# A Fourier layer and a maxout feed-forward on one core: when the last batch's z is split and inverted, and how its sums are spread over the steps

## The chip, the core and the metric

The kernel runs on one core of a Trainium2 chip. The metric is the device time of one execution in microseconds (us): median 1740.72 of three runs, lowest 1739.53, highest 1741.87.

## What is computed

x has shape (8, 3072, 256). Each batch goes through a real Fourier transform along its 3072 positions, a complex 256 x 256 product with bias, a soft threshold of 0.01 and the inverse transform. The 24576 rows that result go through a maxout feed-forward of width 768.

```python
X = np.fft.rfft(x, axis=1)
Yr, Yi = Xr @ w_r - Xi @ w_i + b_r, Xr @ w_i + Xi @ w_r + b_i
Y = soft(Yr, 0.01) + 1j * soft(Yi, 0.01)
y = np.fft.irfft(Y, n=3072, axis=1).reshape(24576, 256)
h = np.maximum(np.maximum(y @ w1, y @ w2), y @ w3)
out = h @ w_out
```

## The kernel before, in words

**Numbers in two halves.** [...] A float32 operand is split into a high half (ScalarE, `activation` with Copy) and a low half (VectorE, operand minus high half), and a product is made of three matmuls: high x high, high x low, low x high.

**Loops.** The main loop (L1427 to L1489) runs over 8 batches b, 8 units c in each, and 6 steps f in each unit. A unit is a tile of y: 384 positions (4 columns n2 times 96) of 256 features, held as `yh` and `yl`. A step makes 128 of the 768 hidden features of one unit. Beside the steps of batch b, the Fourier stages of later batches run out of a list of `events` with due times; by the last batch (b = 7, the only one in `SEVEN`) there is none of that left.

**From z to y.** The spectrum of a batch lies in DRAM as `z_d`. `load_z` (L1013) brings a unit's part to the tile `zq` (one buffer). `split_z` (L1052) makes the halves `zh` (L177, ScalarE) and `zl` (L178, VectorE) and then has SP copy them between partitions to the two tiles `ze` (L1068): four copies of 48 KB for each piece, and two pieces for a unit of the last batch. `inverse` (L1078) multiplies `ze` with tables: 16 short matmuls to `pi` (L1092) for each of the two halves of the features (h = 0, 1). ScalarE copies the even half to `ye` (L1100), VectorE makes `y32` with two instructions (`halves`, L1106), ScalarE its high half `yh` (L1111) and VectorE the low one `yl` (L1113).

**Seven products in the last batch.** There the two products with w1 and w2 of a step are made of seven quarter-size products (`seven_a`, L1179, and its `part_b`, `part_c`, `part_d`). Four of them take sums of quarters of y: `sums` (L1122) makes t1 to t4 with four subtractions (L1127) in the tile `ty`, converts them in one instruction of 768 elements (L1128, ScalarE) and takes their low halves in one (L1129, VectorE).

**One step of the last batch on TensorE**, in the order in which it is written; "last" is the step before:

- `seven_a`: three matmuls `pf<-y`, three `pf<-ty`; ScalarE copies them out of PSUM (L1190, L1192)
- three matmuls of `down` (`pd<-hh`) for an older step
- `part_c` of the last step: six `pu<-ty`; then VectorE adds (L1203) and ScalarE applies Relu (L1208)
- three matmuls of `down`
- `part_b`: three `pu<-ty`, three `pf<-y`; ScalarE copies (L1197)
- three matmuls of `down`
- `part_d` of the last step: three `pu<-yh` that add to what L1203 has read; then VectorE (L1214, twice), ScalarE (L1220) and VectorE (L1221) make the halves `hh` of the hidden features

In three steps of a unit, `down` also takes six matmuls of y itself (`pd<-gh,yh`).

**What is asked for when.** A step has four points at which `flush` (L154) lets the functions run that were put off with `later`; a function put off at one point runs at the next. In the last batch, the split of the next unit's z is asked for in step 0 after `seven_a`, both pieces at once (L1436); the first half of the inverse at the end of step 3 (L1466), the second in step 4 after `part_b` (L1458). `halves`, `parts` and `sums` follow at the next points, one after the other; t1 to t4 and their conversion stand at the first point of step 5, all together. At the start of a batch (c = 0 of the next batch, `late`) the split is asked for in step 2 and the first inverse in step 4. `in_turn` (L163) keeps an instruction behind the last L1208 (ScalarE) and the last L1214 (VectorE) asked for so far.

The framework that builds the program puts the instructions into the queues of the engines by its own plan; on an engine, what is written later can stand earlier. Each engine then runs its queue in order.

Of the kernel before, what the change touches and what calls it, by code (L numbers as in the profile page):

```python
# [101 lines left out]
def fourier_maxout_kernel(  # L102
# [25 lines left out]
    st = {}  # L128
# [31 lines left out]
    def low(ins):  # L160
        st["low"] = ins
# [887 lines left out]
            )  # L1049
        return yh, yl  # L1050

    def split_z(b, pieces=1):  # L1052
        zh = fft.tile([96, NQ, D], F16, name="zh", bufs=1).rearrange("p n d -> p (n d)")
        zl = fft.tile([96, NQ, D], F16, name="zl", bufs=1).rearrange("p n d -> p (n d)")
        both = [
            fft.tile([P, 2, D], F32, name="ze", tag=tag, bufs=3)[0:96].rearrange("p a d -> p (a d)").bitcast(F16)
            for tag in ("vl", "vh")
        ]
        w = NQ * D // pieces
        for i in range(pieces):  # L1060
            cols = slice(i * w, i * w + w)
            with in_turn():
                split_later(zh[:, cols], zl[:, cols], st["zq"][:, cols], st[b, "su"][0][0:96])

            def move(cols=cols):
                for i, t in enumerate((zh, zl)):
                    for e in range(2):
                        nc.sync.dma_start(  # L1068
                            out=both[e][48 * i:48 * i + 48, cols], in_=t[48 * e:48 * e + 48, cols]
                        )  # L1070

            later(move)
        st["z"] = [t.rearrange("p (n d) -> p n d", n=NQ) for t in both]

    HT = NT // 2
# [2 lines left out]
    def inverse(b, c, y=None, part=(0, KD)):  # L1078
# [7 lines left out]
        for h in range(*part):  # L1086
            py = ff_tile("pi")
            pv = py[:, 0:NT].rearrange("p (e n m) -> p e n m", e=2, n=NQ)
            for e in range(2):
                for n2 in range(NQ):  # L1090
                    for i in range(2):
                        st["mm"] = nc.tensor.matmul(  # L1092
                            pv[:, e, n2], st["z"][e][:, n2, h * P:(h + 1) * P],
                            ga_sb[:, i, e, c * NQ + n2], start=i == 0, stop=i == 1,
                        )
            even, y32 = (
                fft.tile([P, 2, D], F32, name=name, tag=tag, bufs=bufs).rearrange("p a d -> p (a d)")[:, 0:n]
                for name, tag, bufs, n in (("ye", "vh", 3, NT // 2), ("y32", "aj", 2, NT))
            )
            nc.scalar.activation(out=even, in_=py[:, NT // 2:NT], func=AF.Copy, scale=Y_SCALE)  # L1100

            def halves(h=h, even=even, y32=y32, pv=pv):
                ev = even.rearrange("p (n m) -> p n m", n=NQ)
                yv = y32.rearrange("p (e m n) -> p e n m", e=2, n=NQ)
                for e in range(2):
                    nc.vector.scalar_tensor_tensor(  # L1106
                        out=yv[:, e], in0=pv[:, 0], scalar=(1 - 2 * e) * Y_SCALE, in1=ev,
                        op0=ALU.mult, op1=ALU.add,
                    )
                def parts():  # L1110
                    nc.scalar.activation(out=yh[:, h], in_=y32, func=AF.Copy)  # L1111
                    later(lambda: low(
                        nc.vector.tensor_tensor(out=yl[:, h], in0=y32, in1=yh[:, h], op=ALU.subtract)  # L1113
                    ))

                later(parts) if len(ys) > 2 else parts()
                if len(ys) > 2:
                    quarter.append(y32)
                    if h:
                        later(sums)  # L1120

            def sums():  # L1122
                t, th, tl = ys[2:]
                (b11, b12), (b21, b22) = ((v[:, 0:HT], v[:, HT:NT]) for v in quarter)
                t1, t2, t3, t4 = (t[:, i] for i in range(4))
                for o, u, v in ((t1, b12, b11), (t2, b22, t1), (t3, b22, b12), (t4, b21, t2)):
                    nc.vector.tensor_tensor(out=o, in0=u, in1=v, op=ALU.subtract)  # L1127
                nc.scalar.activation(out=th, in_=t, func=AF.Copy)  # L1128
                later(lambda: nc.vector.tensor_tensor(out=tl, in0=t, in1=th, op=ALU.subtract))  # L1129

            later(halves)
        return ys
# [290 lines left out]
    def second():  # L1423
        b, c, f, y, p, _ = open_unit
        behind.append((b, c, f, y, up(y, f, 1, p, b == c == 0)))

    for b in range(NB):  # L1427
        for c in range(NCH):
            nxt = (b, c + 1) if c + 1 < NCH else (b + 1, 0) if b + 1 < NB else None
            for f in range(NF):  # L1430
# [2 lines left out]
                got = seven_a(y, f) if seven else (up(y, f, 0), None)  # L1433
                flush()
                late = nxt and (not nxt[1] or b == c == 0)
                if nxt and f == (2 if late else b == 0 and c == 1):  # L1436
                    split_z(nxt[0], 1 if nxt[1] and nxt[0] not in SEVEN else 2)
                if late and f == 4:
                    y_next = inverse(*nxt, None, (0, 1))
                run_until(pos - 2 / 3)  # L1440
# [14 lines left out]
                    got[0]()  # L1455
                open_unit = b, c, f, y, *got
                flush()
                if nxt and not late and f == 4:  # L1458
                    inverse(*nxt, y_next, (1, KD))
                run_until(pos - 1 / 3)  # L1460
                flush()
# [1 line left out]
                    down(*turn, parts[2])  # L1463
                if was:
                    behind.append((*last[0:4], part_d()))
                if nxt and not late and f == 3:  # L1466
                    y_next = inverse(*nxt, None, (0, 1))
                if late and f == 4:
                    inverse(*nxt, y_next, (1, KD))
# [58 lines left out]
```

## Time and profile before

| | |
|---|---|
| median of three runs | 1740.72 us (1739.53 to 1741.87) |
| the profiled execution's own time | 1741.96 us |
| its span, first to last instruction | 1740.2 us |
| granted TensorE clock | 1.000 over the span |
| TensorE, VectorE, ScalarE, GpSimd busy | 99%, 73%, 68%, 16% of the span |
| last batch, steps | from about 1573.7 us to the end |

The profile gives one execution, in us from the first instruction. Busy time is what an engine's instructions cover. Matmuls overlap in the pipeline, so the record of one is longer than the distance to the next; waits of TensorE are therefore read from distances between starts. A line such as L178 is a line of the kernel; where a helper issues an instruction, it is the helper's line.

### The profile page before, as it was taken

The page shows a single profiled execution, that of the slowest core. Times are in us where ns is not written, and L with a number is a line of the kernel's source. Part 1 is how long each engine was busy: PE and PEld are TensorE (multiplying, and loading weights), DVE is VectorE, ACT ScalarE, POOL GpSimd, SP SyncE. Part 2 cuts the span into 40 slices and gives each one's busy share as a digit, 9 for nine tenths or more (in the row PEclk, how much of TensorE's full clock was granted, in tenths as well). Part 3 has the DMA queues.
Part 4 walks back from the last instruction along what each step waited for, and adds up shares of the span by engine and source line. Part 5 has one row for each costly group of instructions (what it writes and reads, how often), then busy time and mean ns, then how long its engine had stood idle before and what let it go on. Part 6 is the DMA issues. An engine that isn't in the chain of part 4 may idle for free.

```text
span 1740.2 us, 42116 instructions
## 1 busy us (share of the span) xinstructions
PE 1715.5 (99%) x16179; PEld 1278.0 (73%) x16179; DVE 1277.0 (73%) x2712; ACT 1182.9 (68%) x2513; POOL 277.9 (16%) x505
## 2 busy tenths in 40 slices
PE   9999999999999999999999999999999999999998
PEld 4866777677776777777777777777777777778998
DVE  2887787687876888668885688767787467767775
ACT  4777676676766777577765767667776566666775
POOL 1001012112121112112221112211212100110000
PEclk9999999999999999999999999999999999999999
DMA  9866566477646677467766668556763444422121
GB/s 290 250 184 185 161 165 168 136 194 205 165 139 179 162 193 197 125 175 185 182 169 165 166 167 211 153 145 156 182 163 113 122 117 108 127 76 66 56 59 34
DMA packets 203735, 269.61 MB, mean 155 GB/s; under 512 B 31310, under 2 KB 153134, under 8 KB 203438
## 3 DMA queue, kind: packets, MB, share of 16 engines
q1 hardware_dynamic: 171294, 193.34, 43.3%
q0 software_dynamic: 24608, 66.62, 11.9%
q10 hardware_dynamic: 7632, 6.95, 1.4%
q8 instruction: 128, 2.10, 0.5%
q14 instruction: 73, 0.60, 0.1%
HBM read 124.31 MB, written 75.50 MB: 115 GB/s over the span
## 4 chain that ended last, share of the span: by engine, by line
PE 81%; DVE 8%; DMA 6%; ACT 4%; issue 1%; SPq 1%; ACTq 0%; POOL 0%; DVEq 0%; POOLq 0%
PE pu L183 11%; PE pu L185 11%; PE pu L184 11%; PE pd L183 8%; PE pd L185 8%; PE pd L184 8%; PE py L183 3%; PE py L185 3%; PE py L184 3%; PE pi L1092 3%; PE px L793 2%; PE pu L1177 2%; PE pa L624 2%; PE pz L961 2%; PE pf L1177 1%
## 5 line engine op out<-in xcount | busy, mean ns | idle before, releaser
L183 PE MATMUL pu<-yh,wuh 128*128 128x384 f16 x1344 | 438.6, 326 | 0.2 <-ACT pu L1143 0.2
L185 PE MATMUL pu<-yh,wul 128*128 128x384 f16 x1344 | 438.0, 326 | 0.0
L184 PE MATMUL pu<-yl,wuh 128*128 128x384 f16 x1344 | 438.0, 326 | 0.0
L183 PE MATMUL pd<-woh,hh 128*128 128x256 f16 x1152 | 314.1, 273 | 0.2 <-ACT hh L1220 0.2
L184 PE MATMUL pd<-wol,hh 128*128 128x256 f16 x1152 | 313.8, 272 | 0.0
L185 PE MATMUL pd<-woh,hh 128*128 128x256 f16 x1152 | 313.6, 273 | 0.0
L175 DVE TENSOR_TENSOR hh<-h,hh 128x384 f16<-128x384 f32 x336 | 185.6, 553 | 110.2 <-ACT hh L174 109.7
L1143 ACT ACTIVATE pu<-pu 128x384 f32<-128x384 f32 x336 | 160.7, 478 | 144.9 <-PE pu L185 134.9
L174 ACT ACTIVATE hh<-h 128x384 f16<-128x384 f32 x336 | 174.4, 519 | 69.6 <-DVE h L1147 64.5
L185 PEld LDWEIGHTS <-wul 128*128 128x128 f16 x1344 | 131.4, 98 | 86.7
L183 PEld LDWEIGHTS <-wuh 128*128 128x128 f16 x1344 | 131.3, 98 | 83.2 <-issue 21.6
L634 POOL DMA_DIRECT2D a_d<-aq x160 | 94.9, 597 | 585.6 <-ACT aq L631 583.2
L184 PEld LDWEIGHTS <-wuh 128*128 128x128 f16 x1344 | 131.4, 98 | 62.9 <-issue 1.4
L1279 POOL DMA_DIRECT2D out_dram<-o x189 | 104.4, 559 | 448.0 <-ACT o L1274 445.3
L1151 ACT ACTIVATE h<-pu 128x384 f32<-128x384 f32 x226 | 109.5, 484 | 48.3 <-PE pu L185 42.8
L183 PE MATMUL py<-wch,tt 128*128 128x256 f16 x504 | 137.3, 273 | 1.8 <-DVE y L1106 0.8
L185 PE MATMUL py<-wch,tt 128*128 128x256 f16 x504 | 137.3, 272 | 0.0
L184 PE MATMUL py<-wcl,tt 128*128 128x256 f16 x504 | 137.3, 272 | 0.0
L183 PEld LDWEIGHTS <-hh 128*128 128x128 f16 x1152 | 112.6, 98 | 33.2 <-issue 11.8
L184 PEld LDWEIGHTS <-hh 128*128 128x128 f16 x1152 | 112.7, 98 | 20.9
L1106 DVE SCALAR_TENSOR_TENSOR y<-pi,ye 128x192 f32<-128x192 f32 x252 | 110.4, 505 | 20.7 <-ACT ye L1100 20.5
L185 PEld LDWEIGHTS <-hh 128*128 128x128 f16 x1152 | 112.6, 98 | 13.8 <-DVE hh L175 0.4
(296 smaller groups left out, 3565.7 us busy)
## 6 DMA issues: line engine op xcount, KB each, us to landing
zq<-z_d SPq DMA_DIRECT2D x63, 384.0 KB, 4.7
out_dram<-o POOLq DMA_DIRECT2D x189, 128.0 KB, 3.5
ab<-a_d SPq DMA_DIRECT2D x84, 256.0 KB, 4.3
ab<-ab SPq DMA_DIRECT2D x336, 64.0 KB, 3.0
vb<-vb SPq DMA_DIRECT2D x308, 64.0 KB, 2.9
z_d<-zs POOLq DMA_DIRECT2D x70, 256.0 KB, 3.8
xm<-in_x_dram SPq DMA_DIRECT2D x40, 384.0 KB, 4.1
a_d<-aq POOLq DMA_DIRECT2D x160, 96.0 KB, 3.4
```

Source lines behind the costliest of these rows:

```text
L174: nc.scalar.activation(out=hi, in_=src, func=AF.Copy)
L175: later(lambda: nc.vector.tensor_tensor(out=lo, in0=src, in1=h, op=ALU.subtract))
L183: nc.tensor.matmul(o, lh, rh, start=start, stop=False, **kw)
L184: nc.tensor.matmul(o, lh, rl, start=False, stop=False, **kw)
L185: st["mm"] = nc.tensor.matmul(o, ll, rh, start=False, stop=stop, **kw)
L634: nc.gpsimd.dma_start(out=av[1 - r, :, :, n:n + 512], in_=o[64 * h:64 * h + 48])
L1092: st["mm"] = nc.tensor.matmul(pv[:, e, n2], st["z"][e][:, n2, h * P:(h + 1) * P], ga_sb[:, i, e, c * NQ + n2], start=i == 0, stop=i == 1,)
L1106: nc.vector.scalar_tensor_tensor(out=yv[:, e], in0=pv[:, 0], scalar=(1 - 2 * e) * Y_SCALE, in1=ev, op0=ALU.mult, op1=ALU.add,)
L1143: st["act"] = nc.scalar.activation(out=p, in_=p, func=AF.Relu)
L1151: st["act"] = nc.scalar.activation(out=h32, in_=p, func=AF.Relu, scale=H_SCALE)
L1177: nc.tensor.matmul(o, w[i], v[j], start=first and n == 0, stop=n == 2, skip_group_check=True)
L1279: nc.gpsimd.dma_start(out=out_v[b, c, t + i], in_=o[:, i])
```

## The change

The diff touches `split_z`, the inner functions of `inverse`, and three conditions of the main loop. `sooner` is true for the units 1 to 7 of the last batch. Their split of z is asked for in step 1, the first piece after `seven_a`, the second piece at the next point. The two halves of the inverse are asked for at the end of step 2 and in step 3. After `halves`, `second` asks for the high half of y and some of the sums, `third` for the low half and the rest; `high_sums` converts the four sums in two instructions of 384 elements, and `low_sums` takes the low halves in two. For unit 0 of the last batch the times of split and inverse stay.

```diff
--- before.py
+++ after.py
@@ -1049,7 +1049,7 @@
             )
         return yh, yl
 
-    def split_z(b, pieces=1):
+    def split_z(b, pieces=1, spread=False):
         zh = fft.tile([96, NQ, D], F16, name="zh", bufs=1).rearrange("p n d -> p (n d)")
         zl = fft.tile([96, NQ, D], F16, name="zl", bufs=1).rearrange("p n d -> p (n d)")
         both = [
@@ -1057,12 +1057,14 @@
             for tag in ("vl", "vh")
         ]
         w = NQ * D // pieces
-        for i in range(pieces):
+        zq = st["zq"]
+
+        def piece(i):
             cols = slice(i * w, i * w + w)
             with in_turn():
-                split_later(zh[:, cols], zl[:, cols], st["zq"][:, cols], st[b, "su"][0][0:96])
-
-            def move(cols=cols):
+                split_later(zh[:, cols], zl[:, cols], zq[:, cols], st[b, "su"][0][0:96])
+
+            def move():
                 for i, t in enumerate((zh, zl)):
                     for e in range(2):
                         nc.sync.dma_start(
@@ -1070,6 +1072,11 @@
                         )
 
             later(move)
+            if spread and i + 1 < pieces:
+                later(lambda: piece(i + 1))
+
+        for i in range(1 if spread else pieces):
+            piece(i)
         st["z"] = [t.rearrange("p (n d) -> p n d", n=NQ) for t in both]
 
     HT = NT // 2
@@ -1107,26 +1114,62 @@
                         out=yv[:, e], in0=pv[:, 0], scalar=(1 - 2 * e) * Y_SCALE, in1=ev,
                         op0=ALU.mult, op1=ALU.add,
                     )
+
+                def high():
+                    nc.scalar.activation(out=yh[:, h], in_=y32, func=AF.Copy)
+
                 def parts():
-                    nc.scalar.activation(out=yh[:, h], in_=y32, func=AF.Copy)
-                    later(lambda: low(
-                        nc.vector.tensor_tensor(out=yl[:, h], in0=y32, in1=yh[:, h], op=ALU.subtract)
-                    ))
-
-                later(parts) if len(ys) > 2 else parts()
-                if len(ys) > 2:
-                    quarter.append(y32)
+                    low(nc.vector.tensor_tensor(out=yl[:, h], in0=y32, in1=yh[:, h], op=ALU.subtract))
+
+                if len(ys) == 2:
+                    high()
+                    later(parts)
+                    return
+                quarter.append(y32)
+
+                def second():
+                    high()
+                    if h and not c:
+                        sums(1, 2, 3)
+                        later(parts)
+                        high_sums()
+                        return
+                    sums(*((1, 2) if h else (0,)))
+                    later(third)
+
+                def third():
+                    parts()
                     if h:
-                        later(sums)
-
-            def sums():
+                        sums(3)
+                        later(high_sums)
+
+                later(second)
+
+            def sums(*which):
+                t = ys[2]
+                b11, b12 = (quarter[0][:, e * HT:e * HT + HT] for e in range(2))
+                b21, b22 = (quarter[-1][:, e * HT:e * HT + HT] for e in range(2))
+                t1, t2, t3, t4 = (t[:, i] for i in range(4))
+                for n in which:
+                    o, u, v = ((t1, b12, b11), (t2, b22, t1), (t3, b22, b12), (t4, b21, t2))[n]
+                    nc.vector.tensor_tensor(out=o, in0=u, in1=v, op=ALU.subtract)
+
+            def high_sums():
                 t, th, tl = ys[2:]
-                (b11, b12), (b21, b22) = ((v[:, 0:HT], v[:, HT:NT]) for v in quarter)
-                t1, t2, t3, t4 = (t[:, i] for i in range(4))
-                for o, u, v in ((t1, b12, b11), (t2, b22, t1), (t3, b22, b12), (t4, b21, t2)):
-                    nc.vector.tensor_tensor(out=o, in0=u, in1=v, op=ALU.subtract)
-                nc.scalar.activation(out=th, in_=t, func=AF.Copy)
-                later(lambda: nc.vector.tensor_tensor(out=tl, in0=t, in1=th, op=ALU.subtract))
+                for q in (slice(2, 4), slice(0, 2)):
+                    nc.scalar.activation(out=th[:, q], in_=t[:, q], func=AF.Copy)
+
+                def low_sums(q):
+                    nc.vector.tensor_tensor(out=tl[:, q], in0=t[:, q], in1=th[:, q], op=ALU.subtract)
+
+                def first():
+                    low_sums(slice(2, 4))
+                    if c:
+                        later(lambda: low_sums(slice(0, 2)))
+                    else:
+                        low_sums(slice(0, 2))
+
+                later(first)
 
             later(halves)
         return ys
@@ -1433,8 +1476,9 @@
                 got = seven_a(y, f) if seven else (up(y, f, 0), None)
                 flush()
                 late = nxt and (not nxt[1] or b == c == 0)
-                if nxt and f == (2 if late else b == 0 and c == 1):
-                    split_z(nxt[0], 1 if nxt[1] and nxt[0] not in SEVEN else 2)
+                sooner = nxt and nxt[0] in SEVEN and not late
+                if nxt and f == (2 if late else 1 if sooner else b == 0 and c == 1):
+                    split_z(nxt[0], 1 if nxt[1] and nxt[0] not in SEVEN else 2, sooner)
                 if late and f == 4:
                     y_next = inverse(*nxt, None, (0, 1))
                 run_until(pos - 2 / 3)
@@ -1455,7 +1499,7 @@
                     got[0]()
                 open_unit = b, c, f, y, *got
                 flush()
-                if nxt and not late and f == 4:
+                if nxt and not late and f == 4 - sooner:
                     inverse(*nxt, y_next, (1, KD))
                 run_until(pos - 1 / 3)
                 flush()
@@ -1463,7 +1507,7 @@
                     down(*turn, parts[2])
                 if was:
                     behind.append((*last[0:4], part_d()))
-                if nxt and not late and f == 3:
+                if nxt and not late and f == 3 - sooner:
                     y_next = inverse(*nxt, None, (0, 1))
                 if late and f == 4:
                     inverse(*nxt, y_next, (1, KD))
```

## Rows read from the trace of the kernel before

**Rows 1.** The page, part 1: busy us (share of the span) and instructions

```profile
PE 1715.5 (99%) x16179; PEld 1278.0 (73%) x16179; DVE 1277.0 (73%) x2712; ACT 1182.9 (68%) x2513; POOL 277.9 (16%) x505
```

**Rows 2.** Stretches: us; busy PE, PEld, DVE, ACT, POOL; clock, DMA share, GB/s

```profile
1600.00:1650.00 50.00, 49.32 (x597) 46.27 (x595) 37.26 (x92) 36.14 (x98) 4.91 (x9) 1.00 0.23 67
```

**Rows 3.** Timeline of TensorE, steps 2 and 3: start us, us, engine, line

```profile
1619.41 0.25 PE L1177 MATMUL pf<-yh,wuh 128*128 128x192 f16 x1
...
1619.66 0.41 PE L1177 MATMUL pf<-ty,aq 128*128 128x192 f16 x3
...
1622.13 0.25 PE L1177 MATMUL pf<-yh,wuh 128*128 128x192 f16 x1
...
1625.50 0.56 PE L1092 MATMUL pi<-ga_sb,ze 96*128 96x48 f16 x16
1625.90 0.24 PE L1177 MATMUL pf<-yh,wuh 128*128 128x192 f16 x1
```

**Rows 4.** Instructions of ty: count, ns min/median/max, first and last start us

```profile
L1129 DVE TENSOR_TENSOR ty<-ty x8: 947/948/957, 1573.3 to 1712.5; 128x768 f16<-128x768 f32 x8
```

**Rows 5.** Timeline of TensorE around the end of the first unit

```profile
1612.80 0.27 PE L185 MATMUL pd<-gh,yl 128*128 128x256 f16 x1
1613.15 0.33 PE L1177 MATMUL pu<-yh,aq 128*128 128x192 f16 x2
...
1613.65 0.61 PE L1177 MATMUL pf<-ty,aq 128*128 128x192 f16 x3
...
1616.32 0.33 PE L1177 MATMUL pf<-ty,aq 128*128 128x192 f16 x2
1616.86 0.33 PE L1177 MATMUL pu<-yh,aq 128*128 128x192 f16 x2 [0.22 <-DVE h L1203]
```

**Rows 6.** Timeline of VectorE over the same end of a unit

```profile
1608.48 0.35 DVE L1127 TENSOR_TENSOR ty<-y 128x192 f32<-128x192 f32 x1
...
1611.51 0.55 DVE L1113 TENSOR_TENSOR yl<-y,yh 128x384 f16<-128x384 f32 x1
...
1612.55 0.55 DVE L1203 TENSOR_TENSOR h<-pu,g 128x384 f32<-128x384 f32 x1
1613.02 0.95 DVE L1129 TENSOR_TENSOR ty<-ty 128x768 f16<-128x768 f32 x1
...
1614.41 1.40 DVE L178 SCALAR_TENSOR_TENSOR zl<-zq,s0u,zh 96x512 f16<-96x512 f32 x2
...
1616.26 0.55 DVE L1203 TENSOR_TENSOR h<-pu,g 128x384 f32<-128x384 f32 x1
```

**Rows 7.** Timeline of ScalarE, steps 0 and 1

```profile
1613.13 0.52 ACT L1208 ACTIVATE h<-h 128x384 f32<-128x384 f32 x1
1613.56 1.32 ACT L177 ACTIVATE zh<-zq,s0u 96x512 f16<-96x512 f32 x2
1614.79 0.31 ACT L1190 ACTIVATE pu<-pf 128x192 f32<-128x192 f32 x1
...
1618.81 0.52 ACT L1208 ACTIVATE h<-h 128x384 f32<-128x384 f32 x1 [0.17 <-DVE h L1203]
```

**Rows 8.** SP's copies to ze, step 0; then their landing over the last batch

```profile
1614.30 1.77 SPq L1068 DMA_DIRECT2D ze<-zh  x3
...
1618.07 1.17 SPq L1068 DMA_DIRECT2D ze<-zl  x2
...
DMA to landing us min/median/max: 1.9/1.9/3.4
```

**Rows 9.** Timeline of ScalarE, then TensorE, before the last batch's first unit

```profile
1559.70 1.32 ACT L177 ACTIVATE zh<-zq,s0u 96x512 f16<-96x512 f32 x2
...
1565.63 0.26 PE L1092 MATMUL pi<-ga_sb,ze 96*128 96x48 f16 x4
1566.63 0.61 PE L1092 MATMUL pi<-ga_sb,ze 96*128 96x48 f16 x12 [0.73 <-DMA ze<-zl]
```

**Rows 10.** TensorE's waits over the whole run: us in total, times, longest

```profile
PE pi L1092 <- DMA ze<-zl: 4.9, 9, 1.2
```

## The prediction

> **What bounds the kernel now.** I read the page first: TensorE is busy for 99% of the span [rows 1], so time can be won only where TensorE still waits, and lost wherever it is made to wait. The change touches the last batch alone (for the other batches the new branches give the old order), so next I took the table of stretches: between 1600 and 1650 us TensorE is busy 49.32 of 50 us, VectorE 37.26, ScalarE 36.14, and DMA runs at 0.23 of its share at full clock [rows 2]. The busy share hides short waits, because a matmul's record is longer than its slot. So the pace comes from the timeline of TensorE. A step is one (b, c, f), a unit is six of them. Step 2 of the second unit starts at 1619.41 and step 3 at 1622.13: 2.72 us without a wait. Step 3 ends at 1625.90, 3.77 us; its sixteen inverse matmuls take 0.40 of that, and six matmuls of y for `down` the other 0.65 [rows 3]. A unit holds six such steps, three times those six matmuls and two inverses: 6 x 2.72 + 3 x 0.65 + 2 x 0.40 = 19.07 us. The units actually repeat every (1712.5 - 1573.3) / 7 = 19.89 us, by the starts of the one `ty` subtraction that each has [rows 4]. So 0.82 us per unit is waiting, 7 x 0.82 = 5.7 us in all (0.33% of the time), and no more than this can be won.
>
> The timeline shows where it lies [rows 5]. The matmuls of 1612.80 and 1613.15 start 0.35 apart instead of 0.11: 0.24 lost. The three `pf<-ty` at 1613.65 take 0.61 where three take 0.41 [rows 3]: 0.20 lost. Two `pf<-ty` at 1616.32 take 0.16 to issue, yet the next starts at 1616.86: 0.38 lost. VectorE is behind each [rows 6]: the add of L1203 comes at 1612.55, behind the subtraction for yl of 1611.51; the low parts of the sums (L1129, 0.95 us) come at 1613.02, when the matmuls already want them; and the two zl (L178, 1.40 us) at 1614.41 push the next L1203 to 1616.26.
>
> **The change, part by part.** First, z. The diff asks for its split one step later (f = 1, not 0) and for the inverse one step sooner (ends at f = 2 and inside f = 3, not 3 and 4). From split to inverse there were nearly four steps; two are left. Nothing is added: eight copies of 48 KB per unit go through SP as before, now four behind each half.
>
> What it removes: in step 0 the two zl no longer stand before L1203, so the 0.38 goes. Moving y's and its sums' work to steps 3 and 4 takes the yl and L1129 out of the last moments of step 5, so the 0.24 and the 0.20 go. A unit has about 5 us of VectorE idle time (74% busy by [rows 2]), and step 1, where the zl now fall, has its L1203 after the first zl and before the second. Left over: between nothing (the work fits) and 7 x 0.38 = 2.7 (both zl stand before L1203 in step 1 as they did in step 0). I take nothing, since the second half is now asked for a quarter step later: gain 5.7.
>
> What it adds to instructions: the conversion and subtraction of the sums are cut in two. One subtraction of 768 took 0.95, one of 384 took 0.55 [rows 6], so two cost 1.10, 0.15 more per unit, 1.2 over eight. It is hidden by VectorE's idle time in steps 4 and 5; if that cover were gone, it is the price. The Trainium skill (VectorE: DVE Perf Modes, The TRN2 errata) speaks against such cuts, because every VectorE instruction on SBUF pays a fixed latency; the two rows agree with it. By it alone, as an estimate, the sum below would be 1.2 us higher, still inside the forecast's own range; by the cover that the rows show it is not, and it stands without.
>
> What it makes late: the copies. The high half of z stands behind the L1208 of the step before (that is what `in_turn` asks for). In a step without a jam L1208 starts 0.60 before the next step (1618.81 against 1619.41), and ScalarE's next instruction follows 0.43 behind (1613.13, 1613.56) [rows 3, 7]: the split starts 0.17 before S, the start of step 1. The first copy is issued 0.74 after that (1613.56, 1614.30), and the last of the eight, since SP needs some 0.6 for each, 4.36 after the first (1618.07 and half of 1.17); a copy lands 1.9 after it is issued [rows 7, 8]. So the last two land at S + 6.24 and S + 6.83. TensorE comes to the inverse at S + 2 x 2.72 = S + 5.44. Its first four matmuls need the first half alone (0.10), the next the seventh copy: 0.70 of waiting. Eight more run, then the eighth copy ends 0.39 more: 1.09 us per unit. The load of the next zq stands behind these copies on SP, as now, and has four steps to spare: nothing.
>
> The trace has this case already, at the start of each batch, where split and inverse are two steps apart too. In the seventh the split starts at 1559.70, the inverse at 1565.63, and after four matmuls the next starts at 1566.63, 0.9 late [rows 9]; TensorE's waits for ze are 4.9 us over nine places, 1.2 at most [rows 10]. There the distance was 5.93, here it is 5.6. So the wait's bounds are: at the lower end nothing, if the builder of the program, which does not keep the written order on an engine (the two `pf<-ty` ahead of the late `pu` belong to the next step, [rows 5]), pulls step 3's matmuls in front; at the upper end 1.5, the 1.2 of [rows 10] with 0.3 allowed for a second, shorter wait in the same inverse. I take 1.0, near the worked 1.09, because in [rows 9] the sixteen stayed in one run and merely waited. Seven units: 7.0 lost.
>
> **Sum.** -5.7 + 7.0 = +1.3 us. The profiled execution took 1741.96 us, 1.8 around its span of 1740.2, and is 1.2 above the median of 1740.72; I put the difference on the median: 1742.0. A difference of 0.2% (3.5 us) is about what a measurement of this kernel can tell from none.
>
> **The rivals.** (A) The forecast: VectorE's waits go, a wait for ze of 0.7 to 1.3 us comes at the first inverse. 1740.7 - 5.7 + 4.9 to 9.1: 1739.9 to 1744.1. (B) The copies are hidden: step 3's first products (0.5 us) and three `pd` (0.33) are put before the matmuls that need the second half. For it: the matmuls pulled forward in [rows 5]. Against: [rows 9]. With 0 to 0.3 left, 1735.0 to 1737.1: faster. (C) Slower: ScalarE takes the first half of z only after the two copies from PSUM of step 1 (L1190, L1192, 0.31 each), as it is written. The first of them waits for the three `pf` of step 1 (0.25 us), so the split starts near S + 0.9, a good 1.0 later, and the wait is 2.1: 1740.7 - 5.7 + 14.7 = 1749.7. It decides from a wait of 1.31 per unit on (a split 0.22 later), where loss passes gain by 3.5. Against it: today the split goes ahead of L1190, 1613.56 against 1614.79 [rows 7]. For it: the second half does have to queue behind them. (D) The change does little: the inverse is planned back to where it is now, the jam before the unit's end stays, and only the zl leave step 0. 0.38 in six units: 1738.4. For it: the first of the four sums already runs at 1608.48, in step 4, though it is asked for in step 5 [rows 6]. Against: the second inverse is asked for a whole step sooner, with nothing to wait for but the first one's buffer.
>
> **How the numbers follow.** A 0.43, B 0.31, C 0.17, D 0.09. The likeliest is A: 1742.0, its own range 1739.9 to 1744.1. The range for 8 in 10 has to reach into B and to the edge of C: 1735.4 to 1745.4, which leaves out the lowest of B and most of C. Faster by over 0.2% (below 1737.2) is B, 0.31; slower by over 0.2% (above 1744.2) is C and the tail of A, 0.18; within is the rest, 0.51.
>
> **What would show it.** In TensorE's waits of the last batch a line pi <- DMA ze with seven places of about 1 us shows A; none shows B. The starts of L1129's successors tell a unit's length: 20.1 us in A, 19.1 in B, 21.2 in C. L1203 should no longer be what `pu` waits for, and the zl should start at least one step after the unit's start; if the zl still stand right before L1203 with a `pu` waiting, my gain is wrong. If the inverse's sixteen matmuls lie apart, mixed with `pf` or `pd`, the builder has reordered and the price of 1.0 is wrong.

## The result and the profile after

The changed kernel takes 1753.72 us (median of 5 runs, 1752.09 to 1758.45), against 1740.72 before. The ratio is 1.0067, with a 95% interval of 1.0051 to 1.0082: slower by 0.67%. The forecast was 1742.0, 1.3 above before and by its own bound of 0.2% most likely no difference, with a range up to 1745.4; the measured time lies above that range. The profiled run took 1754.37 with a span of 1752.6, 12.4 longer than the span of before; these 12.4 us are what has to be found.

The busy time of the engines, from the page of after, is nearly that of before [rows 1]:

```profile
PE 1720.8 (98%) x16179; PEld 1280.4 (73%) x16179; DVE 1279.0 (73%) x2720; ACT 1184.8 (68%) x2521; POOL 278.0 (16%) x505
```

TensorE runs the same 16179 matmuls (its records overlap, so the 5.3 us that they cover in addition are not more work), and no other engine has more to do in any amount that matters. So the time is waiting. The table of stretches over the same 50 us as [rows 2] (us; busy PE, PEld, DVE, ACT, POOL; clock, DMA share, GB/s) shows fewer matmuls, 512 for 597, and a mean granted clock of 0.97 for 1.00:

```profile
1600.00:1650.00 50.00, 45.70 (x512) 41.58 (x509) 34.79 (x85) 33.13 (x90) 4.50 (x9) 0.97 0.21 57
```

TensorE's waits in the last batch, from 1570 on (us in total, times, longest), name the copies of z:

```profile
PE pi L1099 <- DMA ze<-zl: 7.3, 12, 1.2
PE pu L1220 <- DVE h L1246: 1.0, 6, 0.2
PE pd L183 <- ACT hh L1263: 0.2, 1, 0.2
```

The list counts only the idle time that it can put to a releaser. What TensorE really loses is read from its timeline. This is the first inverse of the second unit of the last batch (start us, us, engine, line, op, tiles; idle before):

```profile
1603.66 0.26 PE L1099 MATMUL pi<-ga_sb,ze 96*128 96x48 f16 x4
1604.67 0.38 PE L1099 MATMUL pi<-ga_sb,ze 96*128 96x48 f16 x8 [0.74 <-DMA ze<-zl]
1605.24 0.26 PE L1099 MATMUL pi<-ga_sb,ze 96*128 96x48 f16 x4 [0.19 <-DMA ze<-zl]
1605.35 0.24 PE L1220 MATMUL pf<-yh,wuh 128*128 128x192 f16 x1
```

Four matmuls run on the first half, eight more after the seventh copy, four after the eighth: the pattern of the forecast. From 1603.66 to 1605.35 is 1.69 us, where the sixteen without a wait take 0.40 [rows 3]: 1.29 lost. Read in the same way, the seven units lose 1.20, 1.29, 2.30, 1.11, 1.33, 1.24 and 1.20, in all 9.7 us.

**The rest.** From one first inverse to the next is 21.38 us here (1603.66 to 1625.04), and 21.27, 21.18, 21.42 and 21.35 in four others. Without the wait for ze the five keep 20.1 us on the mean, where a unit of before took 19.89 [rows 4]: 0.2 more, for these five and the last unit, which no inverse follows and which is taken alike, 1.2. The forecast had 0.82 less. The timeline finds the waits, in the second unit: `pu` waits 0.17 for ScalarE's L1233 behind the two zh and 0.27 for VectorE's L1246 behind the two zl (both in step 1); the `pf` after the second inverse waits 0.28 for a PSUM buffer that L1257 holds; at the end of step 4 `pu` waits 0.33 for L1246 again. Their sum is 1.04 (0.82 before), and 19.07 of work + 1.04 + 1.24 of ze is 21.35. The third unit takes 23.62; without its 2.30 this is 21.32, 1.4 above before, and the stretches there show why:

```profile
1625.00:1627.50 2.50, 0.69 (x15) 0.50 (x12) 0.62 (x2) 0.88 (x3) 1.64 (x3) 1.00 0.72 162
1627.50:1629.00 1.50, 1.36 (x12) 1.25 (x13) 0.65 (x2) 0.79 (x3) 0.00 (x0) 0.50 0.67 232
1629.00:1631.00 2.00, 2.00 (x12) 1.46 (x11) 1.41 (x4) 0.91 (x3) 0.00 (x0) 0.52 0.28 90
1631.00:1633.00 2.00, 2.00 (x36) 1.93 (x35) 0.92 (x2) 0.94 (x3) 0.00 (x0) 1.00 0.00 0
```

TensorE is busy 0.69 of 2.5 us; then the granted clock is 0.50, its lower level (1.2 GHz), for 3.4 us, and each stretch holds 12 matmuls where the last has 36. So 9.7 for the copies in seven units, 1.2 for the other waits of six and 1.4 for what else the third took: 12.3 of 12.4.

**The copies' chain.** ScalarE's and SP's timelines, for that second unit (step 1 begins at 1597.81):

```profile
1597.36 0.52 ACT L1251 ACTIVATE h<-h 128x384 f32<-128x384 f32 x1 [0.62 <-DVE h L1246]
1597.79 0.31 ACT L1240 ACTIVATE pu<-pu 128x192 f32<-128x192 f32 x1
1598.04 1.31 ACT L177 ACTIVATE zh<-zq,s0u 96x512 f16<-96x512 f32 x2
1599.26 0.31 ACT L1233 ACTIVATE pu<-pf 128x192 f32<-128x192 f32 x1
```

```profile
1598.77 1.24 SPq L1070 DMA_DIRECT2D ze<-zh  x2
1600.10 1.18 SPq L1070 DMA_DIRECT2D ze<-zl  x2
1601.36 1.18 SPq L1070 DMA_DIRECT2D ze<-zh  x2
1602.63 1.18 SPq L1070 DMA_DIRECT2D ze<-zl  x2
1603.86 0.57 SPq L1018 DMA_DIRECT2D zq<-z_d  x1
```

The eighth copy is issued at 1602.63 + 0.59 = 1603.22; with the 1.9 of landing [rows 8] that is 1605.12, and the last four matmuls come at 1605.24. From the split's start on, the forecast's chain stands to about a tenth (7.00 forecast, 1605.12 - 1598.04 = 7.08 here). But ScalarE's line tells a second thing: the two zh run together (x2 at 1598.04), although the second half is asked for a step part later.

### The profile page after: what moved, and what is told of

Same layout as the page of the kernel before. It is cut to its first block, busy times and chain, and to the rows that moved or that the text cites. A ratio compares the mean times of both kernels' runs of the same rounds, so it can differ in the third digit from the quotient of the medians.

```text
span 1752.6 us, 42138 instructions
## 1 busy us (share of the span) xinstructions
PE 1720.8 (98%) x16179; PEld 1280.4 (73%) x16179; DVE 1279.0 (73%) x2720; ACT 1184.8 (68%) x2521; POOL 278.0 (16%) x505
## 4 chain that ended last, share of the span: by engine, by line
PE 77%; DVE 9%; DMA 7%; ACT 4%; issue 2%; SPq 1%; ACTq 0%; POOL 0%; DVEq 0%; POOLq 0%
PE pu L183 11%; PE pu L185 10%; PE pu L184 10%; PE pd L183 8%; PE pd L185 8%; PE pd L184 8%; PE py L183 3%; PE py L185 3%; PE py L184 3%; PE pi L1099 2%; PE px L793 2%; PE pa L624 2%; DMA ze<-zl 2%; PE pz L961 2%; PE pu L1220 1%
## 5 line engine op out<-in xcount | busy, mean ns | idle before, releaser
L183 PEld LDWEIGHTS <-hh 128*128 128x128 f16 x1152 | 112.7, 98 | 31.8 <-issue 10.5
L184 PEld LDWEIGHTS <-hh 128*128 128x128 f16 x1152 | 112.7, 98 | 21.6 <-issue 0.5
L178 DVE SCALAR_TENSOR_TENSOR zl<-zq,s0u,zh 96x1024 f16<-96x1024 f32 (+1 forms) x77 | 82.6, 1086 | 57.5 <-ACT zh L177 53.1
```

Of the source, the lines that this page charges most:

```text
L178: later(lambda: low(nc.vector.scalar_tensor_tensor(out=lo, in0=src, scalar=scale, in1=h, op0=ALU.mult, op1=ALU.subtract)))
L183: nc.tensor.matmul(o, lh, rh, start=start, stop=False, **kw)
L184: nc.tensor.matmul(o, lh, rl, start=False, stop=False, **kw)
```

## The experiments

Two theories are tried. The copies' theory: the loss is the wait for ze, set by SP's chain of eight issues, against a distance too short for it. The crowd's theory: what the change should have won at VectorE and ScalarE did not come, since the work moved to places just as full. A rival of the second: the new waits come from the PSUM buffer that the sooner inverse holds, not from crowded engines. (The letters A and B in an expectation mean what that expectation says, not the prediction's rivals.) Ratios are to before on the same chip. The times lost per unit are read from TensorE's timeline, as above. Each diff is against the kernel that the run's heading names, or against after where it names none; `...` stands for lines left out.

**e1: the split in step 0 as before, the inverse sooner, new sums.**

```diff
-                if nxt and f == (2 if late else 1 if sooner else b == 0 and c == 1):
+                if nxt and f == (2 if late else b == 0 and c == 1):
```

> The changed kernel with the first half of z's split asked for in step 0 again (second half still one point later, inverse still one step sooner): three steps between split and inverse. Theory (the wait for ze costs the changed kernel some 9.6 us in seven units, the fall of the clock up to 2 more, and the waits for VectorE did not go but moved): no wait pi <- DMA ze in the units 1 to 7, full clock, and about 1.0 us per unit of waits for VectorE and ScalarE left: 1741 to 1743 us. Rival (the new order of the sums is what costs, and the waits for ze only cover waits that would come anyway): 1747 or more. Second rival (the forecast's idea that the sums' spread removes VectorE's waits once the copies are in time): 1735 to 1737.

Measured: 1743.55 (12 runs), ratio 1.0006 (0.9995 to 1.0016). No wait for ze is left. Around the same inverse:

```profile
1604.39 0.56 PE L1099 MATMUL pi<-ga_sb,ze 96*128 96x48 f16 x16
1605.09 0.24 PE L1220 MATMUL pf<-yh,wuh 128*128 128x192 f16 x1
```

All sixteen stand in one run. One step more of distance takes away the loss of the copies and, in the last batch, the fall of the clock: the copies' theory holds. But the next `pf` comes 0.70 later, not 0.40: with L1246 0.34, L1233 0.19 and a second `pf` 0.12, 0.95 per unit are lost, the unit is 20.03, and the 0.82 of before is not won, as the crowd's theory has it.

**e2: the split in step 1, the inverse where it was, new sums.**

```diff
-                if nxt and not late and f == 4 - sooner:
+                if nxt and not late and f == 4:
...
-                if nxt and not late and f == 3 - sooner:
+                if nxt and not late and f == 3:
```

> The changed kernel with the inverse at its old place (end of step 3 and in step 4), the split in step 1 by halves and the new sums kept. Theory: three steps between split and inverse, so no wait for ze; the two zl still run together before the add in step 1 (0.4 us per unit), the end of the unit is as crowded as before the change: 1740 to 1743. Rival (new sums cost by themselves): 1747 or more. If the spread sums do remove the 0.24 and 0.20 at the unit's end: 1737 to 1739.

Measured: 1740.91 (12 runs), 0.9992 (0.9982 to 1.0003). No wait for ze either; 0.24 and 0.27 of the others remain, 0.50 per unit, unit 19.59. The wait for ze thus needs both moves, the later split and the sooner inverse, since e1 and e2 each undo one; the sooner inverse also makes half of the other waits (1.04 in after). The moved split and the new sums together win 0.3 per unit on before.

**e3: before with the new sums alone**, shown against after: the split in step 0, both halves at once, the inverse as before.

```diff
-                if nxt and f == (2 if late else 1 if sooner else b == 0 and c == 1):
-                    split_z(nxt[0], 1 if nxt[1] and nxt[0] not in SEVEN else 2, sooner)
+                if nxt and f == (2 if late else b == 0 and c == 1):
+                    split_z(nxt[0], 1 if nxt[1] and nxt[0] not in SEVEN else 2)
...
-                if nxt and not late and f == 4 - sooner:
+                if nxt and not late and f == 4:
...
-                if nxt and not late and f == 3 - sooner:
+                if nxt and not late and f == 3:
```

> The kernel before with the new sums alone (split in step 0, both pieces at once, inverse at its old place). Theory: their cut into pieces costs or gives within 0.15 us per unit, so 1739 to 1742. Rival (new sums cost by themselves, more instructions on engines that are late): 1744 or more.

Measured: 1741.65 (11 runs), 0.9991 (0.9979 to 1.0003); 0.75 per unit lost, unit 19.83. The cut sums cost nothing that can be seen. Each pair takes 2 x 0.55 for one 0.95, so VectorE does have the 0.15 per unit of fixed latency that the Trainium skill (VectorE: DVE Perf Modes, The TRN2 errata) would charge; the time does not show it.

**e4: the copies of zl on GpSimd's queue**, otherwise after.

```diff
-                        nc.sync.dma_start(
+                        (nc.gpsimd if spread and i else nc.sync).dma_start(
```

> The changed kernel with the copies of zl issued by GpSimd's queue and those of zh by SP's, in the units 1 to 7 of the last batch. Theory (eight issues of 0.6 us one behind another on SP set the landing): the last copy is issued some 2 us sooner, the wait for ze falls from 1.3 to 0.3 us or less per unit: 1742 to 1745. Rival (the landing itself, or the load of zq and the output beside it, sets it): unchanged, 1750 or more.

Measured: 1756.11 (6 runs), 1.0076 (1.0062 to 1.0090). A miss: the time that the copies' theory gave did not come. The two queues, SP's and GpSimd's, do issue the last copies some 1.7 us sooner; in the second unit the eighth copy starts 2.79 us after the first (1595.99), where after has 4.45:

```profile
1596.60 1.81 SPq L1070 DMA_DIRECT2D ze<-zh  x3
1598.52 0.52 SPq L1018 DMA_DIRECT2D zq<-z_d  x1
```

```profile
1597.76 1.52 POOL L1070 DMA_DIRECT2D ze<-zl  x3 [0.19 <-ACT pu L1240]
```

But now the 384 KB of the next zq go out at 1598.52, beside the copies, and the last zl copy (issued 1598.78) lands at 1602.60, 3.8 us later, not 1.9. The waits for ze grow to 9.4 us over 8 places (7.3 in after's list above); by the timeline to 11.1, from 9.7. One wait had hidden another. In the seventh unit, which no load follows, it is another thing: GpSimd's queue waits 2.75 us, by the trace for VectorE's L1264, before it issues the last two copies (1709.21), and 2.0 are lost there.

**e5: e4 with that load asked for one step later.**

```diff
-                if ahead and f == (5 if b == c == 0 else 4 if c == NCH - 1 else 2):
+                if ahead and f == (5 if b == c == 0 else 4 if c == NCH - 1 else 3 if b in SEVEN else 2):
```

> The kernel of the run with two queues (copies of zl on GpSimd's queue), with the load of the next zq in the last batch moved from the end of step 2 to the end of step 3. Theory A (with two queues the copies are issued 2 us sooner, but then the 384 KB load of zq runs beside the last ones and holds them for 3.8 us instead of 1.9): the waits for ze fall from 1.4 to 0.3 us per unit or less, 1743 to 1746 us. Theory B (a copy issued by GpSimd lands late by itself, or TensorE's wait is for something else): waits unchanged, 1752 or more.

Measured: 1757.66 (4 runs), 1.0084 (1.0065 to 1.0103). Inconclusive: the builder issues the load as soon as its buffer is free, whenever it is asked for. SP's queue still has it directly behind the copies:

```profile
1604.51 1.22 SPq L1070 DMA_DIRECT2D ze<-zh  x2
1605.84 0.51 SPq L1018 DMA_DIRECT2D zq<-z_d  x1
```

**e9: e5 with the old zq kept until step 3** by a read of one element on ScalarE, so that the load can't go sooner.

```diff
+                if sooner and f == 3:
+                    with in_turn():
+                        nc.scalar.activation(out=small("held")[0:96], in_=st["zq"][:, 0:1], func=AF.Copy)
```

> Two queues again, and this time the load of the next zq really comes after the inverse: a one-element read of the old zq on ScalarE in step 3 keeps its buffer taken till then (in the run before, the load was issued as soon as its buffer was free, so nothing had been moved). Theory A (the load of zq beside the last copies holds them): the waits for ze fall from 1.4 to 0.3 us per unit or less, 1743 to 1746 us. Theory B (a copy issued by GpSimd lands late by itself): unchanged, 1752 or more.

Measured: 1750.3 (4 runs), 1.0042 (1.0027 to 1.0058). The load now goes at 1609.22, and in five units of seven the wait for ze is gone; two places are left:

```profile
PE pi L1099 <- DMA ze<-zl: 2.5, 2, 1.6
```

The mechanism holds in these five: with the copies' chain cut and the load out of its way, the inverse no longer waits. In the third unit 1.1 us are lost: its last three copies land after 3.5 to 4.0 us, though no load runs beside them, and the cause is open. In the seventh 2.0 are lost, since GpSimd's queue again waits 2.74 us for L1264 before the last two copies (1707.16). The time is above the 1743 to 1746 expected, since these two waits and 1.28 us per unit of the others stay, and the clock falls once, to 0.50 for 3.4 us from 1709.9.

**e11: the same hold, but all copies on SP** (after, with the load's two lines of e5 and e9).

> The changed kernel with the load of zq held back in the same way and all eight copies on SP. Theory (with one queue it is the eight issues in a row, 5 us of them, that set the landing, and the load stands behind them): the wait for ze stays at 1.1 to 1.3 us per unit, 1750 to 1753; units with a wait over 2 us and a fall of the clock become fewer. Rival (the load of zq sets it here too): the waits fall below 0.6, 1746 or less.

Measured: 1756.28 (4 runs), 1.0074 (1.0058 to 1.0090). The time lies above the 1750 to 1753 expected, but what the run was to tell is clear: the waits for ze stay, 1.1 to 1.6 each, one of 2.2:

```profile
PE pi L1099 <- DMA ze<-zl: 7.9, 12, 1.6
```

So in the changed kernel the load is not at fault; SP's eight issues are. Two queues alone (e4) or the load held alone (e11) do not cover the copies; both together do in five units of seven (e9).

**e6: e1 with the inverse's result in another ring of PSUM buffers**, to try the crowd's rival. In e6 and e8 the kernel's output comes out with other values, and why was not found; the number of instructions is that of e1, so the two are read for their waits alone.

```diff
-            py = ff_tile("pi")
+            py = ps.tile([P, 512], F32, name="pi", tag="up", bufs=3) if b in SEVEN and c else ff_tile("pi")
```

> The run with the split in step 0 and the inverse one step sooner, with the PSUM tile of the inverse (pi, units 1 to 7 of the last batch) taken from the three buffers of pu instead of the three of pf. Theory (a sooner inverse holds the third buffer of pf, so that a later pf has to wait for L1257, 0.30 and 0.12 us per unit): these two waits go, 3 us less, 1739 to 1741 us. Rival (the waits come from VectorE being late at that point, whatever buffer pi has): they come back under another name, within 1 us of 1743.5.

Measured: 1742.14 (12 runs), 1.0005 (0.9995 to 1.0016). Both waits of `pf` that e1 had (0.30 and 0.12) are gone, and yet the unit is 20.02: the wait at the end of step 4 has grown from 0.34 to 0.74. TensorE there:

```profile
1612.19 0.27 PE L185 MATMUL pd<-woh,hh 128*128 128x256 f16 x1
1613.04 0.33 PE L1220 MATMUL pu<-yh,aq 128*128 128x192 f16 x2 [0.58 <-DVE h L1246]
```

Two starts 0.85 apart, for 0.11 without a wait. VectorE's timeline has the work for y and its sums in a row before the add of L1246 that this `pu` waits for:

```profile
1609.65 0.85 DVE L1113 SCALAR_TENSOR_TENSOR y<-pi,ye 128x192 f32<-128x192 f32 x2
...
1611.13 0.55 DVE L1122 TENSOR_TENSOR yl<-y,yh 128x384 f16<-128x384 f32 x1
1611.60 0.35 DVE L1155 TENSOR_TENSOR ty<-y,ty 128x192 f32<-128x192 f32 x1
1611.96 0.56 DVE L1264 SCALAR_TENSOR_TENSOR hh<-h,hh 128x384 f16<-128x384 f32 x1
1612.44 0.55 DVE L1246 TENSOR_TENSOR h<-pu,g 128x384 f32<-128x384 f32 x1
```

The buffer was only where the wait showed; with one to spare, the lost time per unit is the same. The rival falls.

**e7: e2 with the second half of z asked for in step 2**, so that the halves stand apart.

```diff
-            if spread and i + 1 < pieces:
-                later(lambda: piece(i + 1))
...
+        st["piece"] = piece
...
+                if sooner and f == 2:
+                    st["piece"](1)
```

> The run with the inverse at its old place, with the second half of z's split asked for in step 2 instead of one point after the first. Theory (the builder put both halves side by side, so that 1.33 us of zl stood before the add of step 1 and cost 0.265 us per unit): that wait goes or halves, 1 to 2 us less than the run it comes from, 1738 to 1740; the inverse still finds its copies. Rival (one zl before an add is enough for the wait): no change, 1741.

Measured: **1739.02** (12 runs, 1736.11 to 1742.64), **0.9982 (0.9970 to 0.9993)**: faster than both kernels. The lost time is 0.24 + 0.08 = 0.32 per unit, the unit 19.39. VectorE's timeline shows what the distance does:

```profile
1614.16 0.75 DVE L178 SCALAR_TENSOR_TENSOR zl<-zq,s0u,zh 96x512 f16<-96x512 f32 x1 [0.24 <-ACT zh L177]
1614.83 0.55 DVE L1263 SCALAR_TENSOR_TENSOR hh<-h,hh 128x384 f16<-128x384 f32 x1
1615.30 0.55 DVE L1245 TENSOR_TENSOR h<-pu,g 128x384 f32<-128x384 f32 x1
...
1617.05 0.75 DVE L178 SCALAR_TENSOR_TENSOR zl<-zq,s0u,zh 96x512 f16<-96x512 f32 x1
```

One zl stands before the add that `pu` waits for (L1245), not two, and TensorE loses 0.08 there. In the changed kernel, where the halves are asked for "later", VectorE has them together in front of the same add (L1246):

```profile
1620.15 1.41 DVE L178 SCALAR_TENSOR_TENSOR zl<-zq,s0u,zh 96x512 f16<-96x512 f32 x2 [0.24 <-ACT zh L177]
1621.48 0.55 DVE L1246 TENSOR_TENSOR h<-pu,g 128x384 f32<-128x384 f32 x1
```

and TensorE's `pd` and the `pu` behind it start 0.37 apart, for 0.11:

```profile
1621.71 0.27 PE L185 MATMUL pd<-woh,hh 128*128 128x256 f16 x1
1622.08 0.32 PE L1220 MATMUL pu<-yh,aq 128*128 128x192 f16 x2
```

**e8: e6 with the halves in steps 0 and 1**, the inverse still sooner.

```diff
-            if spread and i + 1 < pieces:
-                later(lambda: piece(i + 1))
...
+        st["piece"] = piece
...
+                if sooner and f == 1:
+                    st["piece"](1)
```

> All of it together: inverse one step sooner with pi in the buffers of pu, first half of the split in step 0 and the second in step 1. If the three theories hold (copies need over 7 us from the split, buffers of pf, both halves side by side), the copies are in time and what is left are the waits of VectorE at the end of step 4: 1737 to 1739, faster than both kernels. If the sooner inverse only moves the crowd on VectorE: 1740 to 1743.

Measured: 1742.04 (12 runs), 0.9996 (0.9987 to 1.0005). A miss, if the sooner inverse was to pay once the copies were covered: the 0.72 at the end of step 4 stays, 0.80 per unit, unit 19.86 (one unit waits 0.6 for ze besides). The waits list has the same seven places:

```profile
PE pu L1219 <- DVE h L1245: 3.8, 7, 0.6
```

With the copies covered, the halves apart and a buffer to spare, the sooner inverse still wins nothing; it moves the crowd.

**e10: e7 with the subtraction for yl on GpSimd**, after the 0.24 that e7 still loses behind yl.

```diff
-                    low(nc.vector.tensor_tensor(out=yl[:, h], in0=y32, in1=yh[:, h], op=ALU.subtract))
+                    low((nc.gpsimd if b in SEVEN and c else nc.vector).tensor_tensor(out=yl[:, h], in0=y32, in1=yh[:, h], op=ALU.subtract))
```

> The run with the halves of the split in steps 1 and 2, with the low half of y (two subtractions of 384 per unit, units 1 to 7 of the last batch) on GpSimd instead of VectorE. Theory (what is left at the end of a unit, 0.24 us, is VectorE's crowd, in which yl stands before the add of L1245): the 0.24 goes, 1.5 us less than that run, 1736 to 1738 us. Rival (GpSimd's subtraction is slow or holds VectorE up, so that y comes late): 1740 or more.

Measured: 1744.99 (12 runs), 1.0007 (0.9997 to 1.0017). A miss, in the rival's range: the 0.24 went, but `pu` now waits for ScalarE's L1232 and at three other places, 0.46 + 0.16 + 0.27 + 0.09 per unit, and two units wait 0.2 and 1.0 for ze. GpSimd's own rows:

```profile
1590.42 0.91 POOL L1121 TENSOR_TENSOR yl<-y,yh 128x384 f16<-128x384 f32 x1 [4.92 <-ACT yh L1118]
1592.83 1.12 POOL L1121 TENSOR_TENSOR yl<-y,yh 128x384 f16<-128x384 f32 x1 [1.50 <-ACT yh L1118]
```

The same subtraction takes 0.55 on VectorE; the Trainium skill (GPSIMD Engine Reference, Engine selection) has GpSimd about two times slower for two inputs, and the rows agree (1.7 and 2.0 times). ScalarE's L1232 stands behind L1262 in e10 (1616.54, 1616.11), where e7 has it ahead (1611.33, 1611.90); that the wait comes from this order was not tried.

**e12: before with the halves in steps 1 and 2 alone**, old sums, old inverse: which part of e7 wins?

```diff
...
+        for i in range(1 if spread else pieces):
+            piece(i)
+        st["piece"] = piece
...
-                if nxt and f == (2 if late else b == 0 and c == 1):
-                    split_z(nxt[0], 1 if nxt[1] and nxt[0] not in SEVEN else 2)
+                sooner = nxt and nxt[0] in SEVEN and not late
+                if nxt and f == (2 if late else 1 if sooner else b == 0 and c == 1):
+                    split_z(nxt[0], 1 if nxt[1] and nxt[0] not in SEVEN else 2, sooner)
+                if sooner and f == 2:
+                    st["piece"](1)
```

> The kernel before with one thing changed: the split of z by halves, the first asked for in step 1 and the second in step 2; inverse and sums as they were. Theory (the gain of the best version comes from taking the two zl out of step 0 and apart, 0.38 us in six units less 0.08, and the new sums add the 0.20 of the late low parts): 1.8 us below the kernel before, ratio 0.9985 to 0.9995, between the kernel before and the best version. Rival (the new sums carry the gain): no faster than before, ratio 0.9995 to 1.0010. Second rival (the new sums do nothing): as fast as the best version, 0.9982.

Measured: 1742.0 (12 runs), 0.9994 (0.9981 to 1.0006): by time alone it can't be told from no change, nor from e7's ratio. By the trace it loses 0.24 + 0.21 + 0.08 = 0.53 per unit, unit 19.59. So the halves in two steps bring 0.82 to 0.53, and the new sums, with them, 0.53 to 0.32.

The units' lengths agree with 19.07 us of work and what each loses:

| kernel | lost at VectorE, ScalarE, buffers | lost for ze | sum with 19.07 | unit | ratio |
|---|---|---|---|---|---|
| before | 0.82 | 0 | 19.89 | 19.89 | 1 |
| after | 1.04 | 1.24 | 21.35 | 21.3 | 1.0067 |
| e10 | 0.98 | 0 | 20.05 | 20.05 | 1.0007 |
| e1 | 0.95 | 0 | 20.02 | 20.03 | 1.0006 |
| e6 | 0.93 | 0 | 20.00 | 20.02 | 1.0005 |
| e8 | 0.80 | 0 | 19.87 | 19.86 | 0.9996 |
| e3 | 0.75 | 0 | 19.82 | 19.83 | 0.9991 |
| e12 | 0.53 | 0 | 19.60 | 19.59 | 0.9994 |
| e2 | 0.50 | 0 | 19.57 | 19.59 | 0.9992 |
| e7 | 0.32 | 0 | 19.39 | 19.39 | 0.9982 |

(The 19.07 is the prediction's sum of steps, from before's trace; the lost times are read from each kernel's own. For after, the third unit with its slow clock is left out of the means. e7, e8 and e12 have one wait for ze each in the whole batch, 0.5, 0.6 and 0.75, and e10 has the two named; these units are left out too.)

## Why the prediction was wrong

**The step that failed** is "I take nothing, since the second half is now asked for a quarter step later: gain 5.7". In place of a gain of 0.82 per unit came a loss of 0.2: the waits went from 0.82 to 1.04. Of the 11.1 us between the forecast's +1.3 and the 12.4 measured, this step makes 5.7 + 1.2, the copies 2.7 and the rest of the third unit 1.4.

Three things were behind the step. First, the program's builder sets the halves side by side, asked for apart or not (two zl at 1620.15), so step 1 has the jam that step 0 had, 0.27; e7 parts them by a step and it shrinks to 0.08. The text had the price of this, "7 x 0.38 = 2.7", as the upper bound, and chose the lower end on a word of the diff instead of a row. The two zh, side by side ahead of L1233 (1598.04, 1599.26), add 0.17. Second, taking yl and the sums "out of the last moments of step 5" was counted as their vanishing; they became due in steps 3 and 4, where L1246 is as tight (0.33 in after, 0.74 in e6). VectorE's 26% of idle time hid none of it, for what counts is what stands ahead of one add. Third, the inverse takes a buffer of the ring that `pf` uses, and the next `pf` waits for another that L1257 has to free (0.28 in after, 0.30 in e1): not in the text at all. By e6 this is the same lateness in another place, since with a buffer to spare as much is lost before L1246.

The 5.7 was a ceiling of what can be won, and the forecast took the ceiling.

**The term that was too small** is the wait for ze, 7.0 for 9.7. Six of the seven lose 1.23 on the mean, not 1.0; the worked 1.09 was nearer, and rounding it down, toward the 0.9 of the seventh batch, was the wrong way. The split starts 0.23 after the step begins, not 0.17 before it: L1251 starts 0.45 before the step, not 0.60, and L1240 gets in between (1597.79). TensorE came later too, after its two other waits in step 1 (0.17 and 0.27), and this gave some 0.4 back. The third unit's 2.3 was beyond the upper bound of 1.5.

SP's timeline for that unit:

```profile
1622.64 1.75 SPq L1070 DMA_DIRECT2D ze<-zh  x2
1624.49 1.18 SPq L1070 DMA_DIRECT2D ze<-zl  x2
```

One pair of issues took 1.75, not 1.18, and the last copy, issued at 1625.08, lets TensorE go on only at 1627.64, some 2.5 us later where 1.9 is usual: 0.5 to 0.6 us late at each, which makes 2.3 of 1.24. Why that unit's copies were late stays open.

**What was not priced** is the clock: the third unit's long wait is followed by 3.4 us at the lower level, and that unit keeps 1.4 above before's length beside its wait. This is not in every execution: of the five, the one of 1752.09 has a mean granted clock of 1.000, and such a fall takes 0.001 off it.

**What held.** The copies' chain (0.6 per issue, 1.9 to land, four then eight then four matmuls), that the builder leaves the sixteen together and they wait, as the batch starts had shown [rows 9] (so B, where `pf` and `pd` slip in between, did not come), that the distance and the chain of issues make this wait (e1 and e2 take it away by more distance, e9 in five units of seven by a shorter chain), the price of the cut sums (none in e3), and that no more than 0.82 per unit is there to win: no kernel here won more than 0.50.

**The rivals.** Unit lengths of 20.1, 19.1 and 21.2 were to tell A, B and C apart, and the measured 21.3 looks like C. It is not: in C the split waits for L1190 (L1233 after), and that stands at 1599.26, behind the zh of 1598.04. The length is the sum of A's wait, 1.24, and 1.04 of waits that A, B and C had all set to nothing. A single sum can't tell rivals apart when they share a wrong term; the named waits could. The bound of 1.31 us from which C was to decide also rested on that gain. D, the inverse planned back to its old place, did not come: its first half stands at 1603.66, ahead of step 3's `pf` at 1605.35.

## What to carry to other kernels

Before the distance between making an operand and using it is cut, count the chain in serial issues of its queue plus one landing, and compare it with the distance in TensorE's time; here 4.4 + 1.9 us from the first copy on did not fit in two steps of 2.72. A wait found at an engine that is a quarter idle is not won by moving work to another step: look at what stands ahead of the one instruction waited for, there and here, and put pieces in different steps if they are to run apart. The waiting time that a trace shows bounds a gain; what goes is another question.

## What the runs showed of the hardware

- After 2.5 us in which TensorE was busy for 0.69, the granted clock fell from 1.00 to 0.50 for 3.4 us (after; e4 and e9 the same length, from 1712.4 and 1709.9, after waits of 2.0). The waits of 1.1 to 1.3 in the other units of after were not followed by such a fall, nor was one of 2.0 in e5 or of 2.2 in e11: the length of the wait alone does not tell.
- A 48 KB copy that lands 1.9 us after its issue takes 3.8 beside a load of 384 KB (e4, second unit; 3.7 to 4.4 in the first six). With the load held (e9), the last copy lands after 1.8 in five of these six units.
- In the third unit of after a packet of a queue that the trace calls "instruction" falls at 1621.3, beside the late copies, and another at 1623.1; e9 and e11 have such packets at their late units too. But others passed without harm: in the fifth unit of after one falls at 1669.0, and the copy issued at 1669.52 lands after 1.9. Whether they are the cause was not tried and stays open.
